# Attention and a squared-relu FFN on one core: the sixth token tile's second layer as seven half-size products, weight sums spread over two tiles, and the last batch's q placed by DMA

## The chip, the cores and the metric

The kernel runs on one core of one Trainium2 chip, in one launch. The metric is the device time of that launch in microseconds (us). The kernel before takes 291.63 us (median of three runs).

## The reference

Attention is computed for 8 batches, 8 heads, 576 positions and a head size of 64. Heads 0 to 3 see a plain window of 32 positions, heads 4 to 7 a dilated one (every fourth of 128 positions). The result, as a matrix of 4608 tokens by 512, goes through two matrix products with a squared relu between them.

```python
masks = [mask_plain if h < H // 2 else mask_dil for h in range(H)]
scores = np.where(masks, scale * q @ k.T, -1e9)
attn = softmax(scores)
x = (attn @ v)                      # as 4608 x 512
h = np.maximum(x @ w_in, 0.0)       # 512 x 2048
out = (h * h) @ w_out               # 2048 x 512
```

## The kernel before

**The work.** The FFN is cut into nine tiles of 512 tokens (tk0 = 512 t, t = 0 to 8; the first two are issued in halves). In this text "sixth tile" is t = 5, "seventh" t = 6. A tile has 16 product groups of the first layer (`mm1`, line 986: four products of 512 columns for each 128 hidden features, then a relu on ACT, line 999, and a square on DVE, line 1002) and 16 groups of the second layer. Groups are numbered g, 32 to a tile: the fifth tile is 128 to 159, the sixth 160 to 191, the seventh 192 to 223.

**Two forms of the second layer.** Tiles before `FAST` take the plain form (`g2`, line 1165): for each of four blocks of 128 tokens, 16 products of 512 columns into one PSUM bank, which ACT copies into `osb` (line 1171) and SP stores. Tiles from `FAST` on take the form of seven half-size products M1 to M7 (`g2_fast`, line 1125): tokens and features are halved, and instead of eight block products there are seven, of 8 x 2 products of 256 columns each, that is 112. It needs sums of the weights (`weigh`, line 1275, eight instructions, into the staging buffers `rb[0]`) and sums of the tile's h (`add_up`, line 1043, into `rb[2]`); two of its last four sums are put off in the seventh tile (`late`, step `Z0`). After a product, `after` (lines 1059 to 1078) copies or adds its bank into `whole`, from which `keep` stores. Squares of such a tile are made for pairs of groups.

**Attention between the groups.** Batch b is worked while the tiles run: for batch 6 (seen from the sixth tile, t = 160 in the code's step table) a "visit" of small quadrant products (`quadrants`, issued at line 376) comes after group 175 and a second one after 183. The first gives scores for two head pairs and the weighted sums of two others; the second does the same and already holds two score pairs of batch 7. A visit of this kind takes four of the four `pf` banks, besides `pa`, `po` and `pd`. After a visit follow exponentials on ACT with masks on DVE (`E`, lines 742 and 747; an `e` does the exponential alone, an `m` the mask alone), the logarithm and the exponential that make the reciprocal (`L`, lines 709 and 710; `X`, line 724), and the product with it on DVE (lines 727 and 731).

**Data for a batch.** k and q of a batch are loaded by POOL, crossed by four DMA transposes on SP (`cross`, line 263, after group 148 for batch 7: k and q of the first 64 positions of each residue, then of the rest), and then placed by DVE copies (`arrange`): `R` the ends for the dilated heads (lines 352 and 355), `K` and `Q` the plain heads' k and q (lines 346 and 344), each in a first part (two heads, for the second visit of the sixth tile) and a second part (for the first visit of the seventh).

**What sets the order.** Every engine runs its instructions in the order in which the code issues them: a list of groups, and a list of steps `(group, order, batch, code)` written out by hand and sorted. There is no planner with costs.

Of the kernel before, what the change touches and what calls it, by code (L numbers as in the profile page):

```python
# [63 lines left out]
def kernel(  # L64
# [9 lines left out]
    nc = tc.nc  # L74
    P = nc.NUM_PARTITIONS
    B, H, S, D = q.shape
# [17 lines left out]
    NT = 512  # L94
    NTILES = NTOK // NT
    XB = 2
    FAST = 6
    PAIRED = 5
    STAGE = (0, 1, 0, 2, 1, 1, 1, 1)
    NATURAL = 3  # L100
# [232 lines left out]
    def arrange(b: int, what: str, g: int, jj: int, e=None, copy=nc.vector.tensor_copy):  # L333

        src, rows = sides[jj], sides[g]
        n = H // 2
        hs = slice(0, n) if e is None else slice(2 * e, 2 * e + 2)  # L340
        if what == "Q" and b == XB:
            copy(qT[rows, 0:2, jj::2, :], qx[b % 2][src, g:4:2, :, :])
        elif what == "Q":
            copy(q_both[rows, hs, jj::2, :], qx[b % 2][src, hs, :, :])
        elif what == "K":
            nc.vector.tensor_copy(
                k_both[rows, g::2, hs, :].rearrange("p i h (c j m) -> p j (h c) i m", c=2, j=2)[:, jj, :, :, :],
                kx[b % 2][src, hs, :, :].rearrange("p h c (i m) -> p (h c) i m", m=16)[:, :, g::2, :],
            )
        else:  # L350
            ms = (slice(128, M), slice(0, 16))[g]
            copy(
                ends[b % 2][rows, 0, :, :].rearrange("p h (r m) -> p h r m", r=RES)[:, :, jj::2, :], qx[b % 2][src, n:, :, ms]
            )
            copy(
                ends[b % 2][rows, 1, :, :].rearrange("p h (m c j) -> p j h c m", c=2, j=2)[:, jj, :, :, :],
                kx[b % 2][src, n:, :, ms],
            )
# [337 lines left out]
    def natural_step(b: int, code: str):  # L696
# [36 lines left out]
                )  # L733
        else:
            g = int(code[2])
            second = g ^ ((b, e) in ((NATURAL, 1), (B - 1, 1)))
            n = 384 if e >= NE // 2 else (448, 384)[g]
            if "m" not in code:
                if not second:
# [212 lines left out]
    def ffn_groups(tk0: int, nt: int):  # L952
# [69 lines left out]
                    late.append(lambda: add_up(*sums_at[u], (1, 3)))  # L1022

        sums_at = {7: (0, 4), 11: (4, 6), 15: (6, 8)}
        visited = tk0 == FAST * NT

        def quarter(f0, f1, high, j):

# [28 lines left out]
        def after(name):  # L1057

            bank = {k: t[:, :, :] for k, t in cur.items()}
            if name == "M1":  # L1060
                nc.scalar.copy(c11, bank["X"])
            elif name == "M5":
                nc.scalar.copy(c22, bank["Y"])
            elif name == "M6":
                nc.scalar.copy(c12, bank["X"])
            elif name == "M3":
                plus(c12, bank["Y"], c12)
                if final:
                    keep(0, HD, DM)
            elif name == "M7":  # L1070
                plus(c22, bank["X"], c22)
                if final:
                    keep(1, HD, DM)
            elif name == "M2":
                plus(c11, bank["Z"], c11)
                keep(0, 0, DM)
# [13 lines left out]
        def w_of(x):  # L1090
# [8 lines left out]
            "M2": ("Z", raw(1, 0), w_raw(1, 0)),  # L1099
            "M4": ("X", raw(1, 1), w_of(3)),  # L1100
        }
        ITEMS = [(name, f, i, 0, HD) for name in PRODUCTS for f in range(NF // 2) for i in range(2)]
        if final:
            last = ITEMS[-NF:]
            one, *two_ = (
                [("M2", f, i, y0, y1) for f in range(NF // 2)]
                for i, y0, y1 in ((0, 0, HD), (1, 0, HD // 2), (1, HD // 2, HD))
            )
            ITEMS[-2 * NF :] = one + last + two_[0] + two_[1]

        def g2_fast(n):

            head_ = 4 * NF
            lo, hi = (8 * n, 8 * n + 8) if n < 8 else (head_ + 6 * n - 48, head_ + 6 * n - 42 if n < 15 else len(ITEMS))
            if n == 0:
                for bank in "YX":
                    cur[bank] = ps_f.tile([P, 2, HD], f32, name="pf")
            for name, f, i, y0, y1 in ITEMS[lo:hi]:
                bank, lhs, rhs = PRODUCTS[name]
                piece = final and name == "M2"  # L1120
                if piece and f == 0:
                    cur.pop(bank, None)
                if bank not in cur:
                    cur[bank] = ps_f.tile([P, 2, HD], f32, name="pf")
                nc.tensor.matmul(  # L1125
                    cur[bank][:, i, y0:y1], lhs(f, i), rhs(f)[:, y0:y1],
                    start=f == 0 and (piece or name in ("M1", "M5", "M2") and i == 0), stop=f == NF // 2 - 1, skip_group_check=True,
                )
# [221 lines left out]
    for b in range(NATURAL, B):  # L1350
# [5 lines left out]
        def expo(e, *at):  # L1356
            steps.extend((y, 1, b, f"E{e}{x}") for x, y in enumerate(at))
# [28 lines left out]
            norm(1, t + 25)  # L1386
        else:
            visit(t + 15, [(b, 3), (b, 1)], [(b, 0), (b, 2)][: 1 + (b >= PAIRED)])
            if after:
                steps.extend((t + 15, 3, b, f"E1{x}") for x in range(2))  # L1390
            else:
                steps.extend((t + 15, 3, b, f"E1{x}e") for x in (1, 0))
                steps.extend((t + 16, 1, b, f"E1{x}m") for x in (1, 0))
                steps.append((t + 16, 2, b, "Z0"))
            if b >= PAIRED:
                norm(2, t + 15)
            expo(3, *[t + 17 - after] * 2)
            norm(0, t + 19 - 2 * after)
            visit(t + 23, [(b + 1, 2), (b + 1, 0)] if after else [], [(b, 1), (b, 3)])
            if after:  # L1400
                steps.extend((t + 23, 3, b + 1, f"E0{x}") for x in range(2))
                steps.extend((t + 27 + 2 * x, 1, b + 1, f"E2{x}") for x in range(2))
            norm(3, t + 23)
            norm(1, t + 25 - after)
# [16 lines left out]
    for g, group in enumerate(groups):  # L1421
# [45 lines left out]
```

## Time and profile before

| | us |
|---|---|
| runs: median (lowest to highest of 3) | 291.63 (291.43 to 292.61) |
| the profiled execution's own time | 293.39 |
| its span, first to last instruction | 291.6 |
| PE busy in the span | 285.7 |
| ACT busy | 187.7 |
| DVE busy | 178.4 |

The clock granted to TensorE averaged 0.998 of full. PE is TensorE's products, PEld its weight loads, DVE is VectorE, ACT is ScalarE, POOL is GpSimd, SP is SyncE, which here only issues DMAs. A row of the chain of waits gives its start in the span, its length, the engine, what it writes and the line; a row of a group gives the number of instructions, the busy time, the mean of one in ns, and the idle time before them with what ended it. A product's mean duration in a group contains its pipeline, so the pace of products is read from the length of a run of them, divided by their number.

### The profile page before, as it was taken

The page shows a single profiled execution, that of the slowest core. Times are in us where ns is not written, and L with a number is a line of the kernel's source. Part 1 is how long each engine was busy: PE and PEld are TensorE (multiplying, and loading weights), DVE is VectorE, ACT ScalarE, POOL GpSimd, SP SyncE. Part 2 cuts the span into 40 slices and gives each one's busy share as a digit, 9 for nine tenths or more (in the row PEclk, how much of TensorE's full clock was granted, in tenths as well). Part 3 has the DMA queues.
Part 4 walks back from the last instruction along what each step waited for, and adds up shares of the span by engine and source line. Part 5 has one row for each costly group of instructions (what it writes and reads, how often), then busy time and mean ns, then how long its engine had stood idle before and what let it go on. Part 6 is the DMA issues. An engine that isn't in the chain of part 4 may idle for free.

```text
span 291.6 us, 8217 instructions
## 1 busy us (share of the span) xinstructions
PE 285.7 (98%) x3377; PEld 180.4 (62%) x3377; DVE 178.4 (61%) x485; ACT 187.7 (64%) x381; POOL 122.8 (42%) x208
## 2 busy tenths in 40 slices
PE   8999999999999999999999999999999999999994
PEld 7679845958755554554555555555557865885684
DVE  1587414555869764688648747985469537623932
ACT  6588725787847855887757775667568646406620
POOL 8677266666272793767496379600000000000000
PEclk9999999999999999999999999999999999999999
DMA  7999999999999989999899999602100030002004
GB/s 116 193 187 212 204 202 202 183 151 172 133 162 218 176 109 221 149 163 136 124 164 203 115 138 200 81 2 74 72 1 2 2 146 0 2 32 112 2 0 144
DMA packets 83924, 35.77 MB, mean 123 GB/s; under 512 B 53168, under 2 KB 79280, under 8 KB 83888
## 3 DMA queue, kind: packets, MB, share of 16 engines
q0 software_dynamic: 49056, 18.49, 58.6%
q1 hardware_dynamic: 34416, 16.41, 26.8%
q8 instruction: 26, 0.43, 0.6%
q10 hardware_dynamic: 416, 0.36, 0.4%
q14 instruction: 10, 0.08, 0.1%
HBM read 37.50 MB, written 9.44 MB: 161 GB/s over the span
## 4 chain that ended last, share of the span: by engine, by line
PE 93%; ACT 2%; DVE 2%; DMA 1%; issue 1%; POOL 0%; POOLq 0%
PE pf L986 43%; PE pf L1165 26%; PE pf L1125 13%; PE po L376 2%; PE pa L376 1%; PE pf L376 1%; DMA kb<-in_k_dram 1%; PE pa L810 1%; PE po L780 1%; PE pd L376 1%; ACT pt L742 1%; ACT rec L724 0%; DVE xT L727 0%; PE pf L840 0%; PE pf L862 0%
## 5 line engine op out<-in xcount | busy, mean ns | idle before, releaser
L986 PE MATMUL pf<-xT,w_in 128*128 128x512 bf16 (+1 forms) x704 | 127.9, 341 | 0.4 <-DVE xT L934 0.3
L986 PEld LDWEIGHTS <-w_in 128*128 128x128 bf16 x704 | 78.2, 114 | 46.2 <-issue 0.9
L999 ACT ACTIVATE h2T<-pf 128x512 bf16<-128x512 f32 x143 | 83.9, 600 | 32.3 <-PE pf L986 32.1
L1165 PE MATMUL pf<-w_out_sb,h2T 128*128 128x512 bf16 x384 | 85.6, 379 | 0.1
L1002 DVE TENSOR_TENSOR h2T<-h2T 128x512 bf16<-128x512 bf16 (+1 forms) x123 | 55.8, 467 | 37.1 <-ACT h2T L999 35.5
L1165 PEld LDWEIGHTS <-h2T 128*128 128x128 bf16 x384 | 36.5, 98 | 42.3
L328 POOL DMA_DIRECT2D vbd<-in_v_dram x80 | 43.3, 567 | 25.3 <-DMA kb<-in_k_dram 13.2
L1171 ACT COPY osb<-pf 128x512 f32<-128x512 f32 x22 | 12.8, 583 | 20.7 <-PE pf L1165 20.7
L1125 PEld LDWEIGHTS <-h2T 128*128 128x128 bf16 x200 | 18.8, 98 | 2.6
L724 ACT ACTIVATE rec<-rec 128x576 f32<-128x576 f32 x24 | 16.4, 682 | 0.7
L182 POOL DMA_DIRECT2D qb<-in_q_dram x19 | 13.7, 722 | 6.2 <-DMA xx<-qb 4.2
L182 POOL DMA_DIRECT2D kb<-in_k_dram x19 | 13.3, 701 | 5.4 <-DMA w_out_sb<-in_moe_w_out_dram 1.7
L204 POOL DMA_DIRECT2D vbd<-in_v_dram x16 | 10.9, 685 | 10.6 <-DMA kb<-in_k_dram 6.1
L1050 DVE TENSOR_TENSOR whole<-pf,whole 128x512 f32<-128x512 f32 (+2 forms) x11 | 6.5, 594 | 13.9 <-PE pf L1125 13.9
L320 POOL DMA_DIRECT2D vbd<-in_v_dram x20 | 12.0, 616 | 7.2 <-DMA vbd<-in_v_dram 4.1
L742 ACT ACTIVATE pt<-pa 128x384 bf16<-128x384 f32 (+1 forms) x26 | 11.7, 498 | 4.9 <-DVE xT L731 4.2
L314 POOL DMA_DIRECT2D vd<-in_v_dram x20 | 12.0, 614 | 3.7 <-DMA vbd<-in_v_dram 2.4
L727 DVE TENSOR_TENSOR xT<-pf,rec 128x512 bf16<-128x512 f32 x11 | 7.6, 690 | 8.2 <-ACT rec L724 8.2
L727 DVE TENSOR_TENSOR xT<-po,rec 128x512 bf16<-128x512 f32 x13 | 9.0, 690 | 5.8 <-ACT rec L724 5.6
L747 DVE TENSOR_TENSOR pt<-pt,mask_f 128x384 bf16<-128x384 bf16 x24 | 8.3, 353 | 5.8 <-ACT pt L742 5.7
L1125 PE MATMUL pf<-w_out_sb,h2T 128*128 128x256 bf16 (+1 forms) x104 | 11.7, 264 | 0.0
L1125 PE MATMUL pf<-kb,h2T 128*128 128x256 bf16 x96 | 11.5, 273 | 0.0
(176 smaller groups left out, 381.1 us busy)
## 6 DMA issues: line engine op xcount, KB each, us to landing
out_dram<-osb SPq DMA_DIRECT2D x24, 128.0 KB, 4.9
out_dram<-osb SPq DMA_DIRECT2D x12, 256.0 KB, 4.3
qb<-in_q_dram POOLq DMA_DIRECT2D x7, 320.0 KB, 9.2
kb<-in_k_dram POOLq DMA_DIRECT2D x7, 320.0 KB, 9.3
vd<-in_v_dram POOLq DMA_DIRECT2D x34, 64.0 KB, 5.0
w_out_sb<-in_moe_w_out_dram POOLq DMA_DIRECT2D x4, 512.0 KB, 13.6
out_dram<-whole SPq DMA_DIRECT2D x4, 512.0 KB, 3.1
qb<-in_q_dram POOLq DMA_DIRECT2D x6, 256.0 KB, 6.4
```

The source lines that it names most:

```text
L182: nc.gpsimd.dma_start(t[p0 : p0 + n, part, h0:h1, :], src[b, h0:h1, t0 : t0 + RES * n, :].rearrange("h (p r) d -> p h (r d)", r=RES),)
L328: nc.gpsimd.dma_start(v_rows[b % 2][p0 + 16 * r : p0 + 16 * r + 16, e, :, :], v[b, 2 * e + hl, :, :].rearrange("(i m r) d -> r m i d", r=R ...
L376: nc.tensor.matmul(out, lhs, rhs, start=begin, stop=True, skip_group_check=True)
L724: nc.scalar.activation(rec[:, :], rec[:, :], ACT.Exp, scale=-1.0)
L727: nc.vector.tensor_tensor(out=tok[:, :, 16:M], in0=byr(o[:, :]), in1=byr(rec[:, 0:512]), op=ALU.mult)
L742: nc.scalar.activation(pt, sp[b, e][g][:, 0:n], ACT.Exp, scale=SCALE)
L986: nc.tensor.matmul(to, w_in_sb[piece][:, kt, c0 : c0 + 509 : 4], rhs, start=(kt == kts[0] and x == 0), stop=(kt == kts[-1] and x == per - ...
L999: nc.scalar.activation(hv, acc[u][:, :].rearrange("p (x n) -> p x n", x=per), ACT.Relu)
L1002: nc.vector.tensor_tensor(out=hv, in0=hv, in1=hv, op=ALU.mult)
L1125: nc.tensor.matmul(cur[bank][:, i, y0:y1], lhs(f, i), rhs(f)[:, y0:y1], start=f == 0 and (piece or name in ("M1", "M5", "M2") and i == 0), ...
L1165: nc.tensor.matmul(cur[m][:, c0:c1], h2[:, f, P * m : P * m + P], w_out_sb[:, f, c0:c1], start=(f == 0), stop=(f == NF - 1),)
L1171: (nc.vector.tensor_copy if last and part == 1 or tk0 == 3 * NT // 2 else nc.scalar.copy)(osb[:, c0:c1], cur[m][:, c0:c1])
```

## The change

1. `FAST` is 5 in place of 6: the sixth tile's second layer takes the form of seven products. For this tile alone (`crowded`) their order is M1, half of M2, M6, the other half of M2, M5, M7, M3, M4, with the banks X for M1, M6 and M5 (adding up), Z for M2, V for M7 and M4, Q for M3; the seventh and later tiles keep M1, M5, M6, M3, M7, M2, M4 with banks X, Y, Z.
2. The eight weight sums, which stood after groups 161 to 168, now stand after groups 129, 131, 133, 135, 137, 160, 161 and 167.
3. In the sixth tile the two put-off sums of h, the order of exponentials and masks after the first visit, and the places of `E3`, `L0` and `X0` follow what the seventh tile has; after the second visit both logarithms come before both `X`.
4. For batch 7 the first part of `K` moves from groups 170 to 172 to groups 162 and 163, `R` from 167 to 170 to 164 and 165; `Q`, both parts, becomes eight DMAs on SP instead of eight DVE copies.

```diff
-    FAST = 6
+    FAST = 5
+    WEIGH = (129, 131, 133, 135, 137, 160, 161, 167)
...
-        if what == "Q" and b == XB:
+        if what == "Q" and b == B - 1:
+            nc.sync.dma_start(q_both[rows, hs, jj::2, :], qx[b % 2][src, hs, :, :])
+        elif what == "Q" and b == XB:
...
-            second = g ^ ((b, e) in ((NATURAL, 1), (B - 1, 1)))
+            second = g ^ ((b, e) in ((NATURAL, 1), (B - 2, 1), (B - 1, 1)))
...
-        visited = tk0 == FAST * NT
+        visited, crowded = FAST * NT <= tk0 <= (FAST + 1) * NT, tk0 == FAST * NT
...
+            elif crowded and name in ("M6", "M5"):
+                nc.scalar.copy(c21 if name == "M6" else c12, bank["X"])
+            elif crowded and name != "M2":
+                to, one, two_ = {"M7": (c22, "V", c12), "M3": (c12, "Q", c12), "M4": (c21, "V", c21)}[name]
+                plus(to, bank[one], two_)
+                if name != "M7":
+                    keep(int(name == "M4"), 0, DM)
...
+            for name, bank in (("M5", "X"), ("M7", "V"), ("M3", "Q"), ("M4", "V")):
+                PRODUCTS[name] = bank, *PRODUCTS[name][1:]
+            fresh, CUTS = "M1 M2 M7 M3", [8 * n if n < 10 else 6 * n + 20 - max(0, n - 12) for n in range(NF)]
...
-            if after:
+            quick = b > FAST
+            if not quick:
                 steps.extend((t + 15, 3, b, f"E1{x}") for x in range(2))
...
-            expo(3, *[t + 17 - after] * 2)
-            norm(0, t + 19 - 2 * after)
+            expo(3, *[t + 16 + quick] * 2)
+            norm(0, t + 17 + 2 * quick)
...
+            if quick and after:
+                steps.extend([(t + 23, 3, b, "L3"), (t + 24, 3, b, "L1"), (t + 25, 0, b, "X3"), (t + 26, 0, b, "X1")])
...
-            steps.append((start + 3 + x // 2 if early else at + x, 1, b, code))
+            steps.append((start + 3 + x // 2 if early else t - 28 + x // 2 if b == B - 1 else at + x, 1, b, code))
...
-                    steps.append((t - 22 + x - (x + 1) // 4, 1, b, code + "0"))
+                    steps.append((t - 30 + x // 2 if b == B - 1 and x < 4 else t - 22 + x - (x + 1) // 4, 1, b, code + "0"))
...
-        if G * (FAST - 1) < g <= G * (FAST - 1) + 8:
-            weigh(g - G * (FAST - 1) - 1)
+        if g in WEIGH:
+            weigh(WEIGH.index(g))
```

More of the change, by code (lines that the diff above doesn't have):

```diff
@@ L1075, in after @@
                 plus(c11, bank["Z"], c11)
-                keep(0, 0, DM)
+                if not crowded:
+                    keep(0, 0, DM)
             elif name == "M4":
@@ L1101, in ffn_groups @@
         }
+        fresh, CUTS = "M1 M5 M2", [8 * n if n < 8 else 6 * n + 16 for n in range(NF)]
         ITEMS = [(name, f, i, 0, HD) for name in PRODUCTS for f in range(NF // 2) for i in range(2)]
+        if crowded:
+            for name, bank in (("M5", "X"), ("M7", "V"), ("M3", "Q"), ("M4", "V")):
+                PRODUCTS[name] = bank, *PRODUCTS[name][1:]
+            fresh, CUTS = "M1 M2 M7 M3", [8 * n if n < 10 else 6 * n + 20 - max(0, n - 12) for n in range(NF)]
+            ITEMS = [
+                (name, f, i, 0, HD)
+                for name, only in (("M1", None), ("M2", 0), ("M6", None), ("M2", 1), ("M5", None), ("M7", None), ("M3", None), ("M4", None))
+                for f in range(NF // 2)
+                for i in range(2)
+                if only in (None, i)
+            ]
         if final:
@@ L1111, in g2_fast @@
         def g2_fast(n):
-            head_ = 4 * NF
-            lo, hi = (8 * n, 8 * n + 8) if n < 8 else (head_ + 6 * n - 48, head_ + 6 * n - 42 if n < 15 else len(ITEMS))
+            lo, hi = (CUTS + [len(ITEMS)])[n : n + 2]
             if n == 0:
-                for bank in "YX":
+                for bank in "ZX" if crowded else "YX":
                     cur[bank] = ps_f.tile([P, 2, HD], f32, name="pf")
@@ L1126, in g2_fast @@
                     cur[bank][:, i, y0:y1], lhs(f, i), rhs(f)[:, y0:y1],
-                    start=f == 0 and (piece or name in ("M1", "M5", "M2") and i == 0), stop=f == NF // 2 - 1, skip_group_check=True,
+                    start=f == 0 and (piece or name in fresh and i == 0), stop=f == NF // 2 - 1, skip_group_check=True,
                 )
@@ L1402 @@
                 steps.extend((t + 27 + 2 * x, 1, b + 1, f"E2{x}") for x in range(2))
-            norm(3, t + 23)
-            norm(1, t + 25 - after)
+            if quick and after:
+                steps.extend([(t + 23, 3, b, "L3"), (t + 24, 3, b, "L1"), (t + 25, 0, b, "X3"), (t + 26, 0, b, "X1")])
+            else:
+                norm(3, t + 23)
+                norm(1, t + 25 - after)
         at = t - (14 if b < PAIRED else 19 if b == PAIRED else 25)
         for x, code in enumerate(("R00", "R01", "R10", "R11")):
-            steps.append((start + 3 + x // 2 if early else at + x, 1, b, code))
+            steps.append((start + 3 + x // 2 if early else t - 28 + x // 2 if b == B - 1 else at + x, 1, b, code))
         for x, code in enumerate(("K00", "K01", "K10", "K11", "Q00", "Q01", "Q10", "Q11")):
```

## The prediction

> **What bounds the kernel now.** I read the page first: which engine is busy for how long, then who stands on the chain that ended last.
>
> ```profile
> span 291.6 us, 8217 instructions
> PE 285.7 (98%) x3377; PEld 180.4 (62%) x3377; DVE 178.4 (61%) x485; ACT 187.7 (64%) x381; POOL 122.8 (42%) x208
> ...
> PE 93%; ACT 2%; DVE 2%; DMA 1%; issue 1%; POOL 0%; POOLq 0%
> ```
>
> TensorE (PE) is 98% busy and makes up 93% of the chain. DVE and ACT, at 61% and 64%, count only where they release a product late. So the question is what PE's own stream loses, and whether it now has to wait. The chain in order of time gives the stretches (start, length, products) of the sixth tile (first three rows), the seventh and the eighth:
>
> ```profile
> 177.13 13.81 PE pf L986 x64
> 192.14 7.01 PE pf L1165 x32
> 200.34 7.01 PE pf L1165 x32
> 207.35 13.81 PE pf L986 x64
> ...
> 222.36 7.09 PE pf L1125 x64
> 230.24 5.37 PE pf L1125 x48
> 235.60 13.81 PE pf L986 x64
> 249.41 12.23 PE pf L1125 x112
> ```
>
> L1165 is the plain second layer: the sixth tile takes two runs of 32 products, 7.01 us each, 219 ns a product, with one attention visit between. L1125 is the second layer by seven half-size products: the seventh tile (with a visit after its 64th product) takes 7.09 + 5.37, the eighth without a visit 12.23. Each run goes straight into the next stretch: PE does not wait there.
>
> **The change part by part.**
>
> *Sixth tile's second layer (FAST = 5).* It removes 64 products of 512 columns, 7.01 + 7.01 = 14.02 us, and adds 112 of 256 columns with the same visit after the 64th. Nearest rows: 7.09 + 5.37 = 12.46 (seventh tile, broken by a visit) and 12.23 (eighth, unbroken). Saved: 1.56 to 1.79 us. The sixth tile has the visit, so I take the broken row and **1.6 us**. All of it is PE's own stream, so all of it reaches the end unless a new wait eats it. For scale, 0.5% of 291.63 is 1.46 us, about what a measurement of this kernel can tell from no change.
>
> *What ACT and DVE get for it.* The groups of DVE by shape, first in the window of the sixth tile (176 to 208 us), then in that of the seventh (207 to 236 us):
>
> ```profile
> L355 DVE COPY kbd<-xx 64x128 bf16<-64x128 bf16 x4 | 1.2, 308 | 0.0
> L1275 DVE TENSOR_TENSOR qb<-w_out_sb 128x1024 bf16<-128x1024 bf16 x2 | 1.4, 684 | 0.0
> L344 DVE COPY qT<-xx 64x576 bf16<-64x576 bf16 x11 | 3.4, 308 | 0.2
> L346 DVE COPY kbd<-xx 64x320 bf16<-64x320 bf16 x4 | 0.9, 234 | 0.1
> L352 DVE COPY kbd<-xx 64x128 bf16<-64x128 bf16 x4 | 0.8, 188 | 0.1
> ```
>
> ```profile
> L1002 DVE TENSOR_TENSOR h2T<-h2T 128x1024 bf16<-128x1024 bf16 x7 | 4.7, 689 | 5.5 <-ACT h2T L999 5.5
> L1050 DVE TENSOR_TENSOR whole<-pf,whole 128x512 f32<-128x512 f32 x3 | 2.1, 689 | 0.8 <-PE pf L1125 0.8
> L1043 DVE TENSOR_TENSOR qb<-h2T 128x512 bf16<-128x512 bf16 x2 | 0.8, 425 | 0.1
> L1043 DVE TENSOR_TENSOR qb<-h2T 128x1024 bf16<-128x1024 bf16 x1 | 0.7, 692 | 0.0
> ```
>
> ACT: four copies of osb become three copies of the same shape (0.58 each in the rows of the first rival), so ACT loses work. DVE gets four sums into `whole` of 0.69 and twelve sums of h (four of 0.69, eight of 0.42). It loses five weight sums (5 x 0.68) to the tile before and eight copies of q (8 x 0.31). None of these end a chain unless late: see the first rival.
>
> *Weight sums in the fifth tile.* Five of 0.68, spread over nine product groups. That tile's squares are read by the plain second layer, whose products of f begin only after all 16 groups; the sixth tile before carries eight such sums in its first layer and its chain row shows no wait. Cost 0; if that cover failed, the fifth tile's first second-layer product would wait for the delayed square.
>
> *Order of exponentials and reciprocals in the sixth tile.* This is the seventh tile's order, with equal counts on ACT and DVE: cost 0 unless ACT is late (first rival).
>
> *Banks.* The second visit takes four banks, two of them those of M2 and M5; M5's copy ends right before it. Before, the osb copy of the second token block had that place, with the same 0.58. Cost 0, bounded by a copy, 0 to 0.6.
>
> *K and ends first, q by DMA.* These copies read crossed data, so they must not run ahead of the transposes. SP's queue in order, and their landing:
>
> ```profile
> 173.44 1.71 SPq L263 DMA_TRANSPOSE xx<-kb  x1
> 175.24 2.03 SPq L263 DMA_TRANSPOSE xx<-qb  x1
> 177.37 4.36 SPq L950 DMA_DIRECT2D out_dram<-osb  x6
> ```
>
> ```profile
> DMA to landing us min/median/max: 4.7/5.3/7.0
> ```
>
> The last k transpose lands by 173.44 + 4.7 to 7.0 = 178.1 to 180.4, the last q one by 179.9 to 182.2. On DVE the copies of k now stand behind the sixth tile's first square and a weight sum: 177.13 + two groups of 0.86 + about 0.9 until the second is rectified + 0.69 + 0.68 = 181.1; the ends follow a square and the copies later, at about 182.5. So I take no wait, bound 0 to 0.5; squares queue behind it, and M1 behind those. The first four q copies issue after the six stores, from 181.8, each at most as long as a transpose there (2.0), so by 190; they are read at the visit at 192.14 + 7.09 = 199.2, which leaves 9 us for the landing. Behind them on SP wait only the tile's own stores, 14 us away. SP gets eight DMAs more, and the sixth tile's four stores of 256 KB become two of 512 KB, whose landing nothing but the reuse of `whole` in the next tile's second layer waits for, over 12 us later. The second four q copies are the second rival.
>
> Sum: 291.6 - 1.6 = 290.0 us of span. That execution itself took 293.39, 1.8 around the span; less 1.6 it would be 291.8. The median of the runs, 291.63, lies 1.76 below that execution; taking the same 1.6 off gives **290.0 us**.
>
> **The rivals.**
>
> *1. DVE late, so ACT late, so PE waits for a bank (part of the gain gone).* In the new order M1, M6 and M5 add up in one bank, so M6 waits until ACT has copied M1 and M5 until it has copied M6, with only half of M2 between: 8 products of 109 ns = 0.87 us. It just fits if ACT is free at once; the seventh tile shows ACT there:
>
> ```profile
> 224.25 0.58 ACT L1061 COPY whole<-pf 128x512 f32<-128x512 f32 x1 [0.31 <-PE pf L1125]
> 224.83 0.87 ACT L742 ACTIVATE pt<-pa 128x384 bf16<-128x384 f32 x2
> 226.00 0.58 ACT L1063 COPY whole<-pf 128x512 f32<-128x512 f32 x1 [0.30 <-PE pf L1125]
> 226.48 0.60 ACT L709 ACTIVATE rec<-pd 128x512 f32<-128x512 f32 x1
> 226.97 0.23 ACT L710 ACTIVATE rec<-pa 128x64 f32<-128x64 f32 x1
> ```
>
> M1's 16 products are issued by 222.36 + 1.75 = 224.1 and its copy starts 0.15 later; 0.15 + 0.58 and a hand-over back of under 0.1 make 0.8 of the 0.87. ACT had 0.31 to spare before it. Before M6's copy ACT has two exponentials (0.87) and two logarithms (0.6, 0.2), about 1.5 us of issue. The exponentials start when DVE has done the reciprocal products of the visit:
>
> ```profile
> 209.74 0.69 DVE L1002 TENSOR_TENSOR h2T<-h2T 128x1024 bf16<-128x1024 bf16 x1 [2.38 <-ACT h2T L999]
> ...
> 221.23 1.35 DVE L1002 TENSOR_TENSOR h2T<-h2T 128x1024 bf16<-128x1024 bf16 x3
> ...
> 223.97 0.69 DVE L727 TENSOR_TENSOR xT<-pf,rec 128x512 bf16<-128x512 f32 x1 [0.47 <-ACT rec L724]
> ```
>
> The seven squares of pairs (128x1024) wait 5.5 us for ACT by their group's row, 2.38 of it before the first: so 3.1 us of idle inside the first layer, and 0.47 before the reciprocal product, 3.6 together. The sixth tile has two weight sums (1.37), four copies of k (0.23 or less, 0.9) and the ends (4 x 0.188 + 4 x 0.308 = 2.0) on top there: 4.3; its third weight sum falls into the idle time before the first square. So DVE comes 0.7 late by plain addition, and some 0.5 since neighbours overlap (the last three squares, 0.69 + 0.42 + 0.42 = 1.53, take 1.35). Then ACT is ready for M6's copy at 224.83 + 1.5 + 0.5 = 226.8 of the seventh tile's clock, and M6 ends 40 products into the layer, at 222.36 + 40 x 0.109 + 0.15 = 226.9. That is a balance within 0.1 us, and each 0.1 more of delay costs PE 0.1. I price it at 0.2 to 1.2 (1.2: one queued reciprocal and a copy as well): **290.2 to 291.2 us**. Against it: the ends and k were priced without any overlap.
>
> *2. The second four q copies land late (slower).* They follow the stores of the tile on SP: store, three copies, store, the last copy. The first store waits for M3's sum: the layer ends at 207.35 - 1.6 = 205.75, M4's 16 products before that begin at 204.0, and the sum adds 0.15 + 0.69, so 204.9. With 0.73 for each store and each copy (the six stores above took 4.36) the last issues after five of them, at 208.6; with 1.0, at 209.9. The seventh tile's visit reads q at 207.35 + 13.81 - 1.6 = 219.6. So it decides at a landing of **10 us**: each us more stalls PE by one, 11.6 us uses up the gain, 13.1 makes the kernel slower by 0.5%, and the longest landing of the page, 13.6, would give **293.6 us**. The rows against it:
>
> ```profile
> out_dram<-osb SPq DMA_DIRECT2D x24, 128.0 KB, 4.9
> kb<-in_k_dram POOLq DMA_DIRECT2D x7, 320.0 KB, 9.3
> w_out_sb<-in_moe_w_out_dram POOLq DMA_DIRECT2D x4, 512.0 KB, 13.6
> ```
>
> A copy is 64 partitions of 4 x 144 bf16, 74 KB in pieces of 288 bytes; only transfers seven times as large, in the crowded start, took over 10 us.
> The Trainium skill ("DMA: Bandwidth & Descriptors", section "Why small descriptors are slow (HBM only)") holds that copies inside SBUF escape the penalty of small pieces, which speaks against this rival; no run here shows such a copy yet.
>
> *3. Half-width products bound by their weight loads (slower).*
>
> ```profile
> L1125 PEld LDWEIGHTS <-h2T x200: 95/98/99, 222.3 to 287.5; 128*128 128x128 bf16 x100
> ```
>
> A load takes 98 ns of the 109 to 111 between products. It decides at 14.02 / 112 = 125 ns a product: above that the seven products lose. In the sixth tile, with attention's loads and DMA beside it, 138 ns would give 15.5 and **293.1 us**; the seventh tile, with the same kind of visit, shows 111.
> The Trainium skill ("TensorE: Matmul & The Clock Gate", "Back-to-back issue gap") gives a sustained 131 ns for 512 columns and 81 for 128. By that, with some 98 for 256 (an estimate between its two), 64 x 131 = 8.4 us would become 112 x 98 = 11.0, a loss of 2.6 us. This trace disagrees, with 219 and 111 ns, and the measurement decides.
>
> *4. The gain is not there because PE was hidden anyway.* If another engine set the pace of the sixth tile, the time would stay at **291.6**. The chain rows above, PE end to end, speak against it.
>
> **How the numbers follow.** Forecast 0.56 (289.6 to 290.2 with the scatter of the runs), rival 1 0.28, rival 2 0.05, rival 3 0.04, rival 4 0.07. Rival 1 lies on the near side of 1.46 only in its first tenth or so, which I count as a little of "faster". Faster by over 0.5%: 0.57; within 0.5%: 0.35 (rest of 1, rival 4, the early part of 2); slower by over 0.5%: 0.08. The range runs from 289.5 (unbroken row, 1.8, less 0.3 of scatter) to 291.2 (the end of rival 1) and leaves out rivals 2 and 3 and most of 4.
>
> **What would show it.** Right: in the changed kernel's chain the sixth tile's second layer stands as x64 near 7.1 and x48 near 5.3, the next first layer 1.6 us earlier, and PE idle nowhere new. Rival 1: idle of PE before the products of M6 or M5 ended by ACT's copies into `whole`, or M1's last products waiting for DVE's squares. Rival 2: PE idle at the attention line in the visits of the sixth and seventh tile, ended by a DMA into qT. Rival 3: products of L1147 over 125 ns apart. A wait of DVE on the transposes before the copies of k would prove me wrong on their order.

## The result, and the profile after

| | before | after |
|---|---|---|
| median of 17 runs (us) | 291.81 | 290.47 |
| lowest to highest | 291.11 to 295.39 | 289.98 to 291.07 |
| profiled execution / its span | 293.39 / 291.6 | 290.09 / 288.2 |

The ratio is 0.9948, with a 95% interval of 0.9928 to 0.9967. That is 1.5 us by the ratio (0.0052 x 291.81), 1.34 by the medians; 290.0 was forecast, with a range of 289.5 to 291.2. All ratios leave out executions in a slower state (one each for k_ends_late, seven_alone, one_more_sum, no_cover and after_beside, 296.64 to 303.53 us), which the medians contain.

The profiled executions lie 3.4 us of span apart, more than the change is worth. The page of the changed kernel, the lines that answer to those of before:

```profile
span 288.2 us, 8325 instructions
PE 282.0 (98%) x3425; PEld 184.0 (64%) x3425; DVE 182.9 (63%) x486; ACT 187.0 (65%) x380; POOL 122.9 (43%) x208
...
PE 91%; ACT 3%; DVE 2%; DMA 1%; issue 1%; POOL 0%; POOLq 0%
```

PE still is the chain. Its stretches in order of time, changed kernel (start, length, products; L989 is the first layer, L1147 the seven products):

```profile
175.25 13.81 PE pf L989 x64
...
190.26 7.09 PE pf L1147 x64
...
198.54 5.34 PE pf L1147 x48
203.88 13.81 PE pf L989 x64
...
218.89 7.09 PE pf L1147 x64
...
226.77 5.36 PE pf L1147 x48
```

The sixth tile now stands as 7.09 + 5.34 = 12.43 us where 14.02 stood, without a wait in it: 1.59 less. The sixth tile's first layer begins at 175.25 here and at 177.13 in the execution of before; from there to the end it is 112.95 us against 114.47, so 1.52 less. The other 1.88 us were lost before the sixth tile, in that one execution of before, which is 2.07 us behind already at its run of 24 first-layer products (it starts at 20.80 there and at 18.73 here); no edit works that early, and the medians do not have it.

**K and ends.** SP's queue, and then DVE's, in the changed kernel:

```profile
171.44 1.46 SPq L264 DMA_TRANSPOSE xx<-kb  x1
173.00 2.02 SPq L264 DMA_TRANSPOSE xx<-qb  x1
175.11 4.49 SPq L953 DMA_DIRECT2D out_dram<-osb  x6
179.77 2.72 SPq L343 DMA_DIRECT2D qT<-xx  x4
...
205.25 2.14 SPq L343 DMA_DIRECT2D qT<-xx  x3
207.49 0.57 SPq L1058 DMA_DIRECT2D out_dram<-whole  x1
208.11 0.62 SPq L343 DMA_DIRECT2D qT<-xx  x1
```

```profile
177.64 0.69 DVE L1005 TENSOR_TENSOR h2T<-h2T 128x1024 bf16<-128x1024 bf16 x1 [1.66 <-ACT h2T L1002]
...
178.86 0.50 DVE L349 COPY kbd<-xx 64x320 bf16<-64x320 bf16 x2
...
180.65 0.25 DVE L355 COPY kbd<-xx 64x128 bf16<-64x128 bf16 x1
180.76 0.29 DVE L358 COPY kbd<-xx 64x128 bf16<-64x128 bf16 x1
```

The DMAs on the tile of the crossed data (`xx`, from 165 to 182 us: the four transposes, which alone take 4.4 to 5.4, and the first four copies of q out of it) have this landing time in the same kernel, and those on the tile of q (`qT`, all eight copies) the one below:

```profile
DMA to landing us min/median/max: 4.0/4.9/5.4
```

```profile
DMA to landing us min/median/max: 2.6/4.3/5.2
```

The copies of k read crossed k alone, whose last transpose is issued from 171.44 and so lands by 176.8; the first copy of k starts at 178.86. The ends read crossed q as well, whose last transpose is issued from 173.00 and lands by 178.4; their first copy starts at 180.65. Neither has idle time ahead of it, and the room is 2 us or more in both. The last q DMA, from 208.11, lands by 213.3; the seventh tile's visit reads q when the first layer ends, at 203.88 + 13.81 = 217.69. That leaves at least 4.4 us.

**The bank.** ACT at the sixth tile's M1 and M6, and DVE's two products with the reciprocal, the second of which releases the exponentials:

```profile
192.15 0.58 ACT L1064 COPY whole<-pf 128x512 f32<-128x512 f32 x1 [0.31 <-PE pf L1147]
193.05 0.87 ACT L745 ACTIVATE pt<-pa 128x384 bf16<-128x384 f32 x2 [0.32 <-DVE xT L734]
193.81 0.60 ACT L712 ACTIVATE rec<-pd 128x512 f32<-128x512 f32 x1
194.28 0.24 ACT L713 ACTIVATE rec<-pa 128x64 f32<-128x64 f32 x1
194.77 0.58 ACT L1066 COPY whole<-pf 128x512 f32<-128x512 f32 x1 [0.24 <-PE pf L1147]
```

```profile
192.20 0.68 DVE L730 TENSOR_TENSOR xT<-pf,rec 128x512 bf16<-128x512 f32 x1
192.81 0.21 DVE L734 TENSOR_TENSOR xT<-pa,rec 128x64 bf16<-128x64 f32 x1
```

The bracket of the copy at 194.77 (M6) is the number to read: ACT waited 0.24 us for PE, not PE for ACT. The seventh tile before had its exponentials at 224.83, 2.47 us after its second layer began (222.36); here they are at 193.05, 2.79 after 190.26. DVE is 0.32 us late, and 0.24 us are left.

### The profile page after: what moved, and what is told of

Read it like the earlier page. It is cut to its first block, busy times and chain, and to the rows that moved or that the text cites. A ratio compares the mean times of both kernels' runs of the same rounds, so it can differ in the third digit from the quotient of the medians.

```text
span 288.2 us, 8325 instructions
## 1 busy us (share of the span) xinstructions
PE 282.0 (98%) x3425; PEld 184.0 (64%) x3425; DVE 182.9 (63%) x486; ACT 187.0 (65%) x380; POOL 122.9 (43%) x208
## 4 chain that ended last, share of the span: by engine, by line
PE 91%; ACT 3%; DVE 2%; DMA 1%; issue 1%; POOL 0%; POOLq 0%
PE pf L989 42%; PE pf L1187 22%; PE pf L1147 17%; PE po L379 2%; PE pf L379 2%; PE pa L379 1%; DMA kb<-in_k_dram 1%; PE pa L813 1%; ACT h2T L1002 1%; PE pf L865 1%; PE pd L379 1%; ACT pt L745 1%; PE po L783 1%; DVE xT L730 0%; ACT rec L727 0%
## 5 line engine op out<-in xcount | busy, mean ns | idle before, releaser
L989 PE MATMUL pf<-xT,w_in 128*128 128x512 bf16 (+1 forms) x704 | 127.9, 341 | 0.0
L989 PEld LDWEIGHTS <-w_in 128*128 128x128 bf16 x704 | 78.2, 114 | 45.5 <-issue 0.5
L1005 DVE TENSOR_TENSOR h2T<-h2T 128x512 bf16<-128x512 bf16 (+1 forms) x116 | 54.5, 486 | 33.2 <-ACT h2T L1002 31.7
L1187 PE MATMUL pf<-w_out_sb,h2T 128*128 128x512 bf16 x320 | 71.5, 379 | 0.1
L1147 PEld LDWEIGHTS <-h2T 128*128 128x128 bf16 x264 | 24.9, 98 | 3.4
L1193 ACT COPY osb<-pf 128x512 f32<-128x512 f32 x18 | 10.5, 583 | 16.6 <-PE pf L1187 16.6
L1053 DVE TENSOR_TENSOR whole<-pf,whole 128x512 f32<-128x512 f32 (+2 forms) x15 | 9.3, 618 | 14.6 <-PE pf L1147 13.8
L1147 PE MATMUL pf<-w_out_sb,h2T 128*128 128x256 bf16 (+1 forms) x136 | 15.5, 266 | 0.0
L1147 PE MATMUL pf<-kb,h2T 128*128 128x256 bf16 x128 | 15.3, 273 | 0.0
L1147 PE MATMUL pf<-qb,qb 128*128 128x256 bf16 x128 | 14.8, 273 | 0.0
L1147 PEld LDWEIGHTS <-qb 128*128 128x128 bf16 x128 | 12.5, 98 | 1.5
```

The costliest lines, as they stand in the source:

```text
L989: nc.tensor.matmul(to, w_in_sb[piece][:, kt, c0 : c0 + 509 : 4], rhs, start=(kt == kts[0] and x == 0), stop=(kt == kts[-1] and x == per - ...
L1005: nc.vector.tensor_tensor(out=hv, in0=hv, in1=hv, op=ALU.mult)
L1147: nc.tensor.matmul(cur[bank][:, i, y0:y1], lhs(f, i), rhs(f)[:, y0:y1], start=f == 0 and (piece or name in fresh and i == 0), stop=f == NF ...
L1187: nc.tensor.matmul(cur[m][:, c0:c1], h2[:, f, P * m : P * m + P], w_out_sb[:, f, c0:c1], start=(f == 0), stop=(f == NF - 1),)
```

## The experiments

Theory A: the seven products bring about 1.6 us, and the other edits bring nothing by themselves but keep DVE and ACT early enough for that. Rival B: the edits bring part of the gain. Rival C: the margin is so wide that the seven products would have brought their gain without the edits. "Stage" is the sixth tile's second layer up to the visit (64 products), 7.09 us in the changed kernel; a row of a stretch of time gives the stretch, its length, the busy time of PE, PEld, DVE, ACT and POOL, TensorE's granted clock, the DMA share and GB/s. Stages, waits and rows are those of one profiled execution of each kernel.

| kernel | median (us), runs | kernel before beside it | ratio (95%) | stage |
|---|---|---|---|---|
| rest_alone | 291.83, 12 | 291.88 | 1.0000 (0.9986 to 1.0014) | plain |
| q_on_dve | 291.76, 10 | 292.02 | 0.9997 (0.9978 to 1.0015) | 8.23 |
| k_ends_late | 292.92, 10 | 292.02 | 1.0023 (1.0007 to 1.0038) | 9.24 |
| weights_late | 296.35, 4 | 292.02 | 1.0157 (1.0093 to 1.0221) | 11.62 |
| weights_late_again | 295.48, 4 | 291.85 | 1.0124 (1.0067 to 1.0180) | 11.87 |
| seven_alone | 295.97, 4 | 292.02 | 1.0097 (1.0065 to 1.0128) | 11.45 |
| one_more_sum | 291.17, 12 | 291.88 | 0.9970 (0.9953 to 0.9987) | 7.31 |
| no_cover | 291.77, 12 | 291.88 | 0.9993 (0.9976 to 1.0011) | 7.92 |
| two_tiles | 289.62, 12 | 291.88 | 0.9936 (0.9914 to 0.9958) | 7.09; fifth tile 9.01 |
| two_tiles_mended | 289.17, 6 | 292.47 | 0.9883 (0.9850 to 0.9916) | 7.09; fifth tile 7.09 |

**rest_alone: weight sums, k, ends and q as in the changed kernel, without the seven products.** Item 3 of the change, the order of exponentials and sums of h, hangs on `FAST` and goes back with it.

```diff
-    FAST = 5
+    FAST = 6
...
-            second = g ^ ((b, e) in ((NATURAL, 1), (B - 2, 1), (B - 1, 1)))
+            second = g ^ ((b, e) in ((NATURAL, 1), (B - 1, 1)))
...
-        visited, crowded = FAST * NT <= tk0 <= (FAST + 1) * NT, tk0 == FAST * NT
+        visited, crowded = tk0 == FAST * NT, False
```

> The changed kernel without the seven products in the sixth tile (its second layer in the plain form again, order of exponentials as before), but with the sums of weights spread over the fifth and sixth tile, k and ends early and q by DMA. Theory A (these edits are worth nothing by themselves): the kernel before within 0.2 us. Rival C (part of the gain of the change comes from them, by a lighter DVE or fewer waits): 0.3 to 1.4 us below the kernel before.

The stretch of the sixth tile's second layer with its visit, first in this kernel, then in the changed one:

```profile
190.43:205.54 15.11, 15.01 (x169) 7.32 (x167) 8.15 (x26) 9.59 (x22) 0.00 (x0) 1.00 0.18 62
```

```profile
190.19:203.72 13.53, 13.53 (x221) 12.04 (x215) 10.94 (x33) 9.58 (x22) 0.00 (x0) 1.00 0.01 2
```

15.11 against 13.53, and the time is that of the kernel before. These edits alone are worth nothing, to within 0.4 us (0.0014 x 291.88); for them rival B falls. The order of item 3 was not run alone.

**q_on_dve: q of the last batch copied by DVE, as before.**

```diff
-        if what == "Q" and b == B - 1:
-            nc.sync.dma_start(q_both[rows, hs, jj::2, :], qx[b % 2][src, hs, :, :])
-        elif what == "Q" and b == XB:
+        if what == "Q" and b == XB:
```

> The changed kernel with one edit undone: the last batch's q is placed by eight DVE copies again (0.31 us each), four of them among the sixth tile's last squares. Theory A (the gain is TensorE's shorter stream alone, and the other edits pay only by keeping DVE inside the little room it has: 0.24 us before M6's copy, some 0.5 before M1's last products): DVE comes 1.2 us late, TensorE waits about 1.0 to 1.3 us inside the second layer of the sixth tile, so the time is 1.0 to 1.3 us above the changed kernel, 0.2 to 0.5 below the kernel before. Rival B (DVE's delay is hidden, the edit is not needed): within 0.2 us of the changed kernel, no new wait of TensorE.

PE's waits from 185 to 215 us, and ACT at the same place as above:

```profile
PE pf L1145 <- ACT whole L1064: 1.0, 1, 1.0
```

```profile
196.75 0.87 ACT L743 ACTIVATE pt<-pa 128x384 bf16<-128x384 f32 x2 [1.84 <-DVE xT L732]
...
198.09 0.62 ACT L1064 COPY whole<-pf 128x512 f32<-128x512 f32 x1
```

This is rival 1 of the prediction in full: DVE late, the exponentials 1.84 us idle for it instead of 0.32, M6's copy behind them without a bracket, and M5's products waiting for the bank. The stage grows by 1.14, and by it some 70% of the gain are gone; the runs, at 0.9997 (0.9978 to 1.0015), can't tell that from all of it. PE waits for no DVE row here: the four copies of 0.31 us that come before the visit (the other four follow after 207 us) cost 1.14 through two other engines.

**k_ends_late: k and the ends of batch 7 at their old places.**

```diff
-            steps.append((start + 3 + x // 2 if early else t - 28 + x // 2 if b == B - 1 else at + x, 1, b, code))
+            steps.append((start + 3 + x // 2 if early else at + x, 1, b, code))
...
-                    steps.append((t - 30 + x // 2 if b == B - 1 and x < 4 else t - 22 + x - (x + 1) // 4, 1, b, code + "0"))
+                    steps.append((t - 22 + x - (x + 1) // 4, 1, b, code + "0"))
```

> The changed kernel with one edit undone: the last batch's k and ends are copied in their old places (k behind groups 170 to 172, ends behind 167 to 170). DVE's work is the same, only later. Theory A: DVE stands idle early in the sixth tile's first layer and does the 2.9 us of copies when squares and sums of h are due; M1's last products wait for squares by about 2 us and M5 for M6's copy by some 0.4 more, so the time is about 2.5 us above the changed kernel, slower than the kernel before by 0.9. Rival B (only the amount of DVE's work counts, not its place): within 0.2 us of the changed kernel.

PE's waits, and DVE's queue in the first layer of the sixth tile:

```profile
PE pf L1147 <- DVE h2T L1005: 1.6, 1, 1.6
```

```profile
179.74 0.69 DVE L1005 TENSOR_TENSOR h2T<-h2T 128x1024 bf16<-128x1024 bf16 x1 [0.43 <-ACT h2T L1002]
181.47 0.69 DVE L1005 TENSOR_TENSOR h2T<-h2T 128x1024 bf16<-128x1024 bf16 x1 [1.03 <-ACT h2T L1002]
183.20 0.69 DVE L1005 TENSOR_TENSOR h2T<-h2T 128x1024 bf16<-128x1024 bf16 x1 [1.03 <-ACT h2T L1002]
```

The copies cost the same in both places. At the old ones DVE idles 0.43 + 1.03 + 1.03 = 2.5 us early, where the squares come slower than it works them, and is 2.5 us late at the end of the layer. The stage grows by 2.15, a little less than the 2.5 that were expected.

**weights_late: all eight weight sums in the sixth tile, and the same kernel a second time.**

```diff
-    WEIGH = (129, 131, 133, 135, 137, 160, 161, 167)
+    WEIGH = (161, 162, 163, 164, 165, 166, 167, 168)
```

> The changed kernel with one edit undone: all eight sums of weights stand behind groups 161 to 168 of the sixth tile again, five more than in the changed kernel, at 0.60 us of issue each. Theory A: DVE 3.0 us later than in the changed kernel, less the room of 0.24 to 0.5; TensorE waits 2.5 to 3.7 us in the sixth tile's second layer, most of it before M1's last products: slower than the kernel before by 1 to 2 us. Rival B (the sums fall into DVE's idle time, as they did in the kernel before): within 0.2 us of the changed kernel.

PE's waits, and TensorE's granted clock (the third number from the end) in stretches behind them:

```profile
PE pf L1147 <- DVE h2T L1005: 2.1, 2, 1.9
```

```profile
199.00:199.30 0.30, 0.27 (x2) 0.11 (x2) 0.30 (x2) 0.00 (x0) 0.00 (x0) 1.00 0.00 0
199.30:200.00 0.70, 0.70 (x7) 0.54 (x6) 0.67 (x3) 0.20 (x1) 0.00 (x0) 0.79 0.00 0
...
201.00:202.00 1.00, 1.00 (x6) 0.73 (x5) 0.96 (x5) 0.67 (x2) 0.00 (x0) 0.50 0.00 0
...
203.00:204.00 1.00, 1.00 (x11) 0.85 (x10) 0.68 (x3) 0.00 (x0) 0.00 (x0) 0.94 0.00 0
```

The waits of M1's products for DVE, read between starts of products less 0.109 each, come to 0.25 + 0.37 + 2.09 = 2.7 us, inside what was expected. The stage grew by 4.53. The rest is in the clock column: half of full speed from about 199.7 to 203.1, products 213 ns apart instead of 109. That was not expected (1 to 2 us slower than the kernel before were, by the ratio it is 4.6), and this execution had a clock of 0.74 in its first 20 us too, so the kernel ran again.

> The same kernel as weights_late, a second time, for one question: there the sixth tile's first 64 second-layer products took 11.62 us, of which 3.0 us were waits for VectorE's combinations, and after the last wait of 2.2 us the products stood 213 ns apart until 203.3 us at a granted clock of 0.59, instead of 109 ns at 1.0. Theory (TensorE's clock is cut after such a wait in this place): waits of about 3.0 us again and about 1.8 us behind them at a clock near 0.6, the stage near 11.6 us. Rival (a throttle of that one execution, which had 0.74 in its first 20 us as well): the same waits, products 109 ns apart right behind them, clock 1.0, the stage near 9.9 to 10.1 us, and the time near 294.5 to 295 us.

```profile
PE pf L1147 <- DVE h2T L1005: 2.5, 3, 1.9
```

```profile
196.00:196.50 0.50, 0.50 (x6) 0.45 (x5) 0.47 (x2) 0.50 (x1) 0.00 (x0) 0.85 0.00 0
196.50:199.00 2.50, 2.50 (x14) 1.76 (x13) 2.46 (x10) 1.48 (x4) 0.00 (x0) 0.50 0.00 0
...
199.50:200.00 0.50, 0.50 (x6) 0.36 (x5) 0.29 (x2) 0.00 (x0) 0.00 (x0) 0.74 0.00 0
```

It came again, at a clock of 1.00 in the first 20 us: waits of 3.0 us, and a halved clock from about 196.35 to 199.76 us, 3.4 us long, so 1.7 us lost. The rival (one odd execution) falls. But not every execution has it: 3.4 us at half speed take the mean clock of a span of 293.7 to 0.994, and three of the eight runs of the two show 1.000. (A mean of 0.994 alone does not place it: one run of the kernel before has that too.)

**seven_alone: the seven products and their order, with q, k, ends and weight sums all as before.** Its edit is the three diffs above together.

> The seven products in the sixth tile alone: q by DVE, k and ends late, and all sums of weights in the sixth tile, as in the kernel before. Theory A: the delays of DVE add up to about 5 us in the sixth tile, TensorE loses all of the 1.6 us and 3 to 3.5 more: 3 to 3.5 us slower than the kernel before (294.8 to 295.3). Rival B (the gain of the shorter stream is independent of the rest): 1.4 us faster than the kernel before, as the changed kernel.

PE's waits from 185 to 215 us:

```profile
PE pf L1145 <- DVE h2T L1003: 2.5, 2, 2.4
PE pf L1145 <- ACT whole L1064: 1.3, 1, 1.3
```

Both waits stand one after the other: the stage grows by 4.36, and the kernel is 2.8 us slower than before (0.0097 x 292.02). Rival C falls. The sum of the single stages (1.14 + 2.15 + 4.53) is larger, 7.8. Part of that is the clock, which did not fall here although PE waited 2.5 us at one place. Part is, by DVE's rows, that the weight sums fill the idle time that late copies leave: after the square at 179.80 DVE has no idle time ahead of an instruction up to the visit's reciprocal product here, where k_ends_late had 2.5 us.

**one_more_sum: the margin, by a dose.** A ninth sum of 0.6 us repeats the first one.

```diff
+        if g == 163:
+            weigh(0)
```

> The changed kernel with one DVE instruction more: the first sum of weights is computed a second time behind group 163 (0.60 us of issue), with the same result. It is a dose for the room that DVE has. Theory A, with a room of 0.24 us: TensorE waits 0.3 to 0.55 us, most of it before M5 for the copy of M6, and the span grows by as much. Rival B (room of over 0.6 us): no wait, within 0.1 us of the changed kernel's span.

ACT in this kernel:

```profile
193.65 0.87 ACT L745 ACTIVATE pt<-pa 128x384 bf16<-128x384 f32 x2 [0.92 <-DVE xT L734]
...
194.88 0.24 ACT L713 ACTIVATE rec<-pa 128x64 f32<-128x64 f32 x1
194.99 0.62 ACT L1066 COPY whole<-pf 128x512 f32<-128x512 f32 x1
```

The exponentials wait 0.92 instead of 0.32, so the whole 0.60 arrives at the exponentials. The stage grows by 0.22, less than the 0.3 to 0.55 that were expected: 0.38 us of the dose were swallowed, which is the margin. It is the bracket of M6's copy, 0.24, and 0.13 more: a copy that stands ready in ACT's queue starts at 194.99, before the logarithm ahead of it ends at 194.88 + 0.24 = 195.12.

**no_cover: M6 right behind M1, without the half of M2 between.**

```diff
-                for name, only in (("M1", None), ("M2", 0), ("M6", None), ("M2", 1), ("M5", None), ("M7", None), ("M3", None), ("M4", None))
+                for name, only in (("M1", None), ("M6", None), ("M2", 0), ("M2", 1), ("M5", None), ("M7", None), ("M3", None), ("M4", None))
```

> The changed kernel with the sixth tile's products in the order M1, M6, M2, M5 (M2 whole, in place of its halves between): M6 then starts in M1's bank with nothing between. Theory A (a bank is free only when ACT's copy has read it: about 0.15 + 0.58 + 0.05 us after the last product's issue is done): TensorE waits 0.8 us before M6, and none before M5: 0.8 us above the changed kernel. Rival B (accumulation goes on while the copy reads, or ACT is ahead): no wait.

```profile
PE pf L1147 <- ACT whole L1064: 0.7, 1, 0.7
```

The stage grows by 0.83, about the 8 x 0.109 = 0.87 us of the cover that was taken away: the two halves of M2 hide a copy each, and just that.

**two_tiles, and two_tiles_mended: the same for the fifth tile as well.** The first kernel has `FAST = 4`, the sums after 97, 98, 99, 101, 103, 128, 129 and 135, q by DMA for the last two batches, `visited` and `crowded` one tile wider, and for batch 6 as for batch 7 k and ends early. Two edits are not shown: the fifth tile's stores are split in halves, and the order of two exponentials of batch 5 follows that of batch 6.

```diff
-    FAST = 5
-    WEIGH = (129, 131, 133, 135, 137, 160, 161, 167)
+    FAST = 4
+    WEIGH = (97, 98, 99, 101, 103, 128, 129, 135)
...
-        if what == "Q" and b == B - 1:
+        if what == "Q" and b >= B - 2:
...
-            steps.append((start + 3 + x // 2 if early else t - 28 + x // 2 if b == B - 1 else at + x, 1, b, code))
+            steps.append((start + 3 + x // 2 if early else t - 28 + x // 2 if b == B - 1 else t - 28 + x // 2 if b == B - 2 else at + x, 1, b, code))
...
-                    steps.append((t - 30 + x // 2 if b == B - 1 and x < 4 else t - 22 + x - (x + 1) // 4, 1, b, code + "0"))
+                    steps.append((t - 30 + x // 2 if b == B - 1 and x < 4 else t - 30 + x // 2 if b == B - 2 and x < 4 else t - 22 + x - (x + 1) // 4, 1, b, code + "0"))
```

> The change carried one tile further: the fifth and the sixth tile both take the seven products with the changed order, the sums of weights stand behind groups 97, 98, 99, 101, 103, 128, 129 and 135, and batch 6 gets k and ends early and q by DMA as batch 7 does. The fifth tile's rows lie in two halves, so its stores are split. Theory A: one more stretch of 14.02 us becomes 12.46 or less, with DVE's room in the fifth tile about that of the sixth: 1.5 us below the changed kernel, 2.9 to 3.1 below the kernel before. Rival D (in the fifth tile, with POOL and its loads still busy and the transposes landing late, DVE comes late and TensorE waits): between the changed kernel and 1 us above it.

PE's waits in the fifth tile, and DVE's queue there:

```profile
PE pf L1149 <- DVE h2T L1005: 1.4, 1, 1.4
```

```profile
152.58 0.19 DVE L355 COPY kbd<-xx 64x128 bf16<-64x128 bf16 x1 [2.00 <-DMA xx<-qb]
```

Its ratio, 0.9936 (0.9914 to 0.9958), overlaps that of the changed kernel, 0.9948 (0.9928 to 0.9967): the two can't be told apart, where 1.5 us less were expected. In the profiled execution (290.87 us, above the median) the fifth tile's second layer takes 9.01 + 5.35 = 14.36, 0.34 more than the plain form's 14.02. DVE stood 2.00 us before the ends, for the last q transpose, with the squares queued behind it. It is the wait that the prediction named for the sixth tile, there before the copies of k ("would prove me wrong on their order"), one tile earlier. So the mended version takes the half of batch 6's ends that reads the last transposes (`R00`, `R01`) behind the landing, the other half one group earlier, and moves one sum from the fifth tile to the fourth; the copies of k stay where they were:

```diff
-    WEIGH = (97, 98, 99, 101, 103, 128, 129, 135)
+    WEIGH = (97, 98, 99, 101, 103, 105, 128, 129)
...
-            steps.append((start + 3 + x // 2 if early else t - 28 + x // 2 if b == B - 1 else t - 28 + x // 2 if b == B - 2 else at + x, 1, b, code))
+            steps.append((start + 3 + x // 2 if early else t - 28 + x // 2 if b == B - 1 else t - 25 if b == B - 2 and x < 2 else t - 28 if b == B - 2 else at + x, 1, b, code))
```

> The second layer by seven half-size products in the fifth and the sixth tile, as in two_tiles, but with batch 6's copies of the ends, and its K copy, put behind the last transposes' landing, and the fifth tile's sums at other groups. Theory (the loss in two_tiles is VectorE's wait of 2.0 us for the last q transpose): VectorE waits for no transpose there, the fifth tile's first 64 products of the second layer take 7.1 us (up to 7.4) instead of 9.01, the sixth tile's stay at 7.09, and the whole lies about 1.9 us below two_tiles by stages: ratio to the kernel before near 0.990, some 3 us below it. Rival: the work moved back only comes together with the later sums and copies, VectorE ends its combinations as late as before, and the stage stays near 9 us; ratio 0.9935, no better than two_tiles. A second rival: the stage is mended, but a fresh wait of 0.4 to 1 us stands ahead of the fifth tile's visit; ratio 0.992.

Its chain (fifth tile, then sixth):

```profile
160.43 7.09 PE pf L1149 x64
...
168.71 5.34 PE pf L1149 x48
...
189.07 7.09 PE pf L1149 x64
...
197.35 5.35 PE pf L1149 x48
```

PE has no wait left in either tile. The edit does not owe this to early transposes: in the profile of mended_beside the last q transpose is issued at 146.94, later than the 145.54 of two_tiles, and the stages are 7.09 again. The edit moves ends and a sum together, so what each brings is not shown apart. Since the median of the kernel before was high beside it (292.47), it ran once more beside the changed kernel:

> The changed kernel once more, so that it and the mended two-tile version stand beside the same runs of the kernel before. Theory (the gain is the sixth tile's 1.5 us): ratio 0.9948 plus or minus 0.001, some 1.5 us below the kernel before.

> The mended two-tile version beside the changed kernel, on the same chip. Theory (each tile's seven products bring the same 1.5 to 1.6 us): 1.5 us below the changed kernel and 3.1 below the kernel before, ratio 0.9895. Rival (part of the 3.3 us of the first run came from slow runs of the kernel before on that chip, and the true gain is smaller): 0.9 us or less below the changed kernel.

On one chip: kernel before 292.35 (14 runs); changed kernel 290.61 (8), ratio 0.9953 (0.9928 to 0.9978); mended version 289.06 (6), ratio 0.9890 (0.9870 to 0.9911). By the medians, 1.7 us for the sixth tile's change and 1.6 for the fifth's; by the ratios, 1.4 and 1.8; by the chains, 1.59 each. This version beats both kernels.

## Why the prediction was right

- **The sum, 1.6 us.** Taken 14.02 - 12.46; measured 14.02 - 12.43 = 1.59 in the chain, 1.5 by the ratio. It was right to take the row that is broken by a visit.
- **Everything else at nothing.** rest_alone shows it for the weight sums, k, ends and q, ratio 1.0000; for the order of item 3 it is argued from the seventh tile, not shown. Costed at nothing does not mean without effect: each of three of these edits, undone alone, costs 1.1 to 4.5 us of the stage (of the 4.5 some 1.7 are the fallen clock). The second visit's banks cost nothing: from the last product before it to the first behind it there are 1.19 us in both kernels (198.54 - 197.35 and 200.34 - 199.15).
- **K and ends without a wait.** Right, with 2.0 us of room for k (178.86 against a landing by 176.8) and 2.2 for the ends (180.65 against 178.4). two_tiles shows the price when it fails: DVE idle 2.00, the stage 1.9 longer.
- **Rival 1, the bank.** Its mechanism is real: q_on_dve, one_more_sum and no_cover each set it off. It did not come because DVE was 0.32 us late, not 0.5 as the sum said (0.7 by plain addition). The working priced ACT ready 0.1 before M6's end; the row says 0.24, the dose 0.38. The miss was on the safe side, and that part was luck: a balance within 0.1 us could have fallen either way, and the chances say no more (0.56 against 0.28). Its reason, "the ends and k were priced without any overlap", fits the row in which four copies of 128 columns start 0.11 apart in pairs, but was not tried alone.
- **Rival 2, q landing late.** The first store came later than the working had it: SP issues it at 204.57 and the second q copies from 205.25, after the layer's end at 203.88, where the first store had been put 0.85 before that end. DVE had the visit's products and copies ahead of M3's sum, which starts at 203.85. From the last issue to the read there are 9.6 us, near the 10 that were named as the limit; the landing, 5.2 at most, decided. No transfer was delayed by an edit, so the price beyond the limit is untried. One argument against this rival was a misreading: not "only transfers seven times as large" took over 10 us. In the same trace four loads of 128 KB into `qb` took 13.8 (their median), four loads of 72 KB 10.1, and the longest transpose 13.1. The copies stayed clear of that here; in two_tiles_mended the four of batch 6, from 148.8, landed only after 4.2 to 8.1 us.
- **Rival 3, half-width products.** 7.09 / 64 = 111 ns in the sixth tile, as in the seventh, not 125.
- **Rival 4.** PE was not hidden: in each of the two tiles 1.59 us came off the chain, and the runs became shorter by 1.4 to 1.8.

## What to carry to other kernels

When a stage is made shorter on the bound engine, the engines that feed it lose that time as cover: count their idle time inside the stage before, in us, and move work out of it until the sum fits. Moving work earlier helps only where the engine idles and where the data is there already: five of the eight sums cost nothing in the tile before, and early copies that outran their transposes cost 1.9 us. Measure the margin by a dose: one extra instruction of known length showed 0.38 us left in a trace, a size that ratios with intervals of 0.4 us and more to each side could not show.

## What the runs showed of the hardware

- **A wait of 2.1 us can be followed by a halved TensorE clock.** In weights_late_again two products stood 2.19 us apart ahead of 195.15, so PE waited 2.1 us out of the 3.4 before 196.35, and the clock was then 0.50 for 3.4 us; in the profile of seven_alone one wait of 2.5 us had no such sequel (clock 1.00 from 188 to 206 us). That the wait is the cause is argued, from the same stretch at the same place in two executions, not shown. The Trainium skill ("TensorE: Matmul & The Clock Gate", section "Part 1: The HAM clock gate") tells of a free-running window of about 3.4 us whose activity sets the clock, half or full. The length here agrees, 3.4 us in both profiles, and a window that starts anywhere would explain why only some executions have it; but by the Trainium skill's section it takes an idle window, and here PE had worked in the 3.4 us before. Which share of idle time decides was not tried.
- **Small copies within SBUF by DMA.** Eight of 72 KB took 0.59 to 0.84 us each on SP's queue and landed 2.6 to 5.2 us after their issue (rows of `qT`: 590/614/837 ns, 2.6/4.3/5.2 us), no slower than the transposes' 4.4 to 5.4 at that place. The prediction named the Trainium skill ("DMA: Bandwidth & Descriptors", section "Why small descriptors are slow (HBM only)") for copies inside SBUF without a penalty for small pieces: nothing here speaks against that, but no copy in larger pieces was run beside these, so no run shows it.
